# A forgetting-attention kernel with an MLP behind it: the first pair's decay folded into its score product, its f rows repeated by a second queue, batch 1's loads reordered, and slot 4's bank and transposes changed

## The chip, the core and the metric

The kernel runs on one core of a Trainium2 chip. A core has TensorE (PE in the profile: matrix products from SBUF into PSUM), VectorE (DVE), ScalarE (ACT), GpSimd (POOL) and SyncE (SP). Each engine takes its own instructions in order; they wait for one another by semaphores. Loads and stores are DMAs, issued here from GpSimd's queue, from SyncE's and, in the changed kernel, once from ScalarE's; all of them share 16 DMA engines. GpSimd's DMAs convert float32 into float16 on the way. The metric is device time of one execution in microseconds (us), lower is better.

## The reference, cut to what matters

Eight batches of eight heads, 576 positions, 64 numbers per head. Attention with a forget gate f comes first; all heads of a position together are then the 512 inputs of an MLP with a hidden width of 2048, over 8 x 576 = 4608 positions.

```python
scores = scale * np.matmul(q, k.transpose(0, 1, 3, 2))
log_f = np.log(np.clip(f, 0.0001, 1.0))
cum = np.cumsum(log_f, axis=-1)
decay = cum[:, :, :, None] - cum[:, :, None, :]
scores = np.where(causal, -1000000000.0, scores + decay)
...
return np.matmul(attn, v)        # attn: softmax of scores
...
h = x @ w_in
g = h - np.tanh(h)
return g @ w_out
```

The decay of a score depends on its query row by cum of the query's position, and on its key column by minus cum of the key's. So it can be had by a few more rows of the q k product: a row of ones against cum, and so on.

## The kernel before, in words

Work goes by pairs of heads: 8 batches of 4 pairs, 32 pairs in all, and the MLP's products are dealt out between the pairs' own work from pair 4 on. The order on all engines is written out by hand: `start` (L562) for the first pair's opening, `bulk` (L193) for loads, and then, for each slot p (L652), the list that `att_items` (L588) makes. A slot holds the scores of pair p, the values of pair p-1, the transposes of q and k for pair p+1, and the loads that the table LOADS (L208) names by slot and tile. Here slot 4 is the one in which batch 0 ends and batch 1 and the MLP begin.

A pair has seven score tiles (`TILES`, L311): three for its first head, a small one for both heads' last key block (tile 3), three for the second head. `scores` (L328) makes a tile: products of KT (keys) with QT (queries) into a PSUM bank (L348), for batch 0 a product that adds the causal mask (L351), and an exp on ScalarE (L357) from PSUM into SBUF. The tag "sc" has two banks, so a tile waits for the exp of two tiles ago; tile 3 of batch 0 and the dummy products (`unread`, L553) use the bank "tr". `values` (L378) multiplies exps by v (L385), and VectorE divides (L394 to L396). `turn` (L403) transposes the result into XR, for batch 0 by TensorE (L411) and a ScalarE copy (L412). `mlp1` (L432) makes a tile of h (L442), ScalarE its tanh (L447), VectorE the sum gq (L453), which frees h's bank. Banks of the MLP, of the turn and of the early transposes come in turn from three (`m_bank`, L70, with the count M_AT).

For batch 0, q and k come in rows (`load_qk`, L101) and are turned by TensorE (`trans`, L266; products L277, copies out of PSUM by ScalarE L288 or VectorE L290). In the first slots nearly all of VectorE's time is these copies.

KT and QT have 67 rows: 64 of data and three for the decay. The decay starts from f, loaded as 64 rows (L135): clamp (L162), Ln (L169), running sum cum by a scan (L171), its float16 upper part chi (L174), the rest clo (L178) and cq (L565). `load_aug` (L180) puts one row each of chi, clo and cq into rows 64 to 66 by DMA, for batch 0 from GpSimd's queue, and `const_rows` (L187) the constant rows from SyncE's. Pair 0 would be too early for that: its scores use 64 rows of KT and QT, and `decay_part` (L316) adds the decay by two more products for each piece, one with the selector sel over chi and clo (L317), one with a column of the identity over cq (L319). A piece is a block of keys against a run of queries; pair 0 has twelve.

GpSimd's queue holds, in this order: q and k of heads 0 to 3, the identity mask between them (L142), v of heads 0 and 1, q of heads 4 to 7, the three decay rows, k of heads 4 to 7, four blocks of v (`load_v_block`, L130), and then batch 1's q and k, w_in in two halves (`load_win`, L200) and batch 1's v.

The dummy products of L556 read nothing of the problem and nobody reads them; they keep TensorE at work while data is on the way.

Of the kernel before, what the change touches and what calls it, by code (L numbers as in the profile page):

```python
# [21 lines left out]
def kernel(  # L22
# [107 lines left out]
    def load_v_block(b, n, h0, h1):  # L130
# [8 lines left out]
    nc.vector.memset(warm, 1.0)  # L139
    id16 = cst.tile([P, P], FP16)  # L140
# [5 lines left out]
    ones16 = TK[0:NH, 0, :]  # L146
    sel = cst.tile([P, 2], FP16)
    dec = cst.tile([P, PITCH], FP16)
# [5 lines left out]
    nc.vector.memset(dec[:, S:PITCH], 0.0)  # L154
# [6 lines left out]

    nc.vector.tensor_scalar(out=lf, in0=lf, scalar1=0.0001, scalar2=1.0,  # L162
                            op0=ALU.max, op1=ALU.min)

    nc.vector.scalar_tensor_tensor(out=sel, in0=id16[:, 0:2], scalar=-1.0, in1=id16[:, NH:NH + 2],
                                   op0=ALU.mult, op1=ALU.subtract)
    nc.vector.memset(vn[0][D:P, NJ - 1, :, :], 0.0)
    nc.vector.memset(vn[0][:, :, :, D:VW], 1.0)
    nc.scalar.activation(out=lf, in_=lf, func=AF.Ln)  # L169
    cum = TQ[0][0:NH, :, :].rearrange("p c s -> p (c s)").bitcast(FP32)[:, S:2 * S]  # L170
    nc.vector.tensor_tensor_scan(out=cum, data0=ones16, data1=lf, initial=0.0,  # L171
                                 op0=ALU.mult, op1=ALU.add)
    chi = dec[0:NH, 0:S]
    nc.vector.tensor_scalar_mul(out=chi, in0=cum, scalar1=inv_qscale)  # L174
    cq = cst.tile([NH, S], FP16)
    expo = cst.tile([1, 1], FP32)
    clo = dec[NH:2 * NH, 0:S]
    nc.vector.scalar_tensor_tensor(out=clo, in0=cum, scalar=inv_qscale, in1=chi,  # L178
                                   op0=ALU.mult, op1=ALU.subtract)
    def load_aug(b):  # L180
        i, hs = b % 2, slice(b * H, (b + 1) * H)
        eng = nc.gpsimd if b == 0 else nc.sync
        eng.dma_start(out=KT[i][D:D + 1, :, 0:S], in_=chi[hs, :])
        eng.dma_start(out=QT[i][D + 2:D + 3, :, :], in_=cq[hs, :])
        eng.dma_start(out=KT[i][D + 1:D + 2, :, 0:S], in_=clo[hs, :])
# [18 lines left out]
    def load_wout(t0, t1):  # L204
# [111 lines left out]
    def decay_part(ps, a, j, i0, n, col):  # L316
        nc.tensor.matmul(out=ps[:, col:col + n], lhsT=dec[:, j * P:(j + 1) * P],  # L317
                         rhs=sel[:, a:a + 1].to_broadcast([P, n]), start=True, stop=False)
        nc.tensor.matmul(out=ps[:, col:col + n], lhsT=id16[0:NH, a:a + 1].to_broadcast([NH, P]),  # L319
                         rhs=cq[:, i0:i0 + n], start=False, stop=False)  # L320

    FIRST = []

    def decay(ti):
        FIRST.append(ps_sc.tile([P, 512], FP32, tag="sc", name="ps"))
        decay_part(FIRST[0], *TILES[ti][0])

    def scores(b, c, ti):  # L328
        if FIRST:
            ps = FIRST.pop()  # L330
        elif b == 0 and ti == LAST:
# [9 lines left out]
        own = b == 0 and c == 0  # L341
        rows = D if own else D + 3
        for a, j, i0, n, col in TILES[ti]:
            h = 2 * c + a
            if own and ti > 0:
                decay_part(ps, a, j, i0, n, col)
            cut = min(P, n) if b == 0 and i0 == j * P else 0
            nc.tensor.matmul(out=ps[:, col:col + n], lhsT=KT[b % 2][0:rows, h, j * P:(j + 1) * P],  # L348
                             rhs=QT[b % 2][0:rows, h, i0:i0 + n], start=not own, stop=cut == 0)
            if cut:  # L350
                nc.tensor.matmul(out=ps[:, col:col + cut], lhsT=id16, rhs=late[:, 0:cut],  # L351
                                 start=False, stop=True)
# [4 lines left out]
        nc.scalar.activation(out=e[:, lo:hi], in_=ps[:, lo:hi], func=AF.Exp, scale=qscale)  # L357
# [204 lines left out]
    def start():  # L562
        unread(33)
        q_rest = trans(*pairs[0], qn, QT, True, "AAAA", True)
        nc.scalar.activation(out=cq, in_=cum, func=AF.Copy, bias=-SHIFT * inv_qscale, scale=inv_qscale)  # L565
        nc.scalar.activation(out=expo, in_=lf[0:1, 0:1], func=AF.Exp)
        unread(6)
        k_rest = trans(*pairs[0], kn, KT, True, "VVVV", True)
        unread(22)
        decay(0)  # L570
        unread(8)
        scores(*pairs[0], 0)
        for fn in k_rest:
            fn()
        q_rest[0]()
        scores(*pairs[0], 1)
        q_rest[1]()
        for e in EL[0:2]:
            nc.vector.memset(e, 0.0)
        nc.vector.memset(KT[0][:, :, S:PITCH], 0.0)  # L580
# [7 lines left out]
    def att_items(p):  # L588
# [8 lines left out]
        for ti in range(len(TILES)):  # L597
# [5 lines left out]
            if early and p > 0 and ti in (0, 6):  # L603
                put(unread, 2)
# [4 lines left out]
            at_q, at_k = (1, 3) if p == 0 else (0, 1) if early else (0, 2) if p == NPAIR else (0, 3)  # L609
# [37 lines left out]
    FIVE = {PE, mybir.EngineType.Pool, mybir.EngineType.SP, mybir.EngineType.DVE, mybir.EngineType.Activation}  # L647
    with tc.manual_schedule(engines=FIVE):
        start()
    with tc.manual_schedule(engines=FIVE):  # L650
        bulk()
        for p in range(len(pairs) + 1):  # L652
            b, c = divmod(p, NPAIR)
            items = att_items(p)
            take = TAKE[p] if p < len(TAKE) else 8 - (p - len(TAKE)) % 2
            if p == 2 * NPAIR - 1:
                keep()
            if p == 2 * NPAIR + 1:
                KEPT.clear()
                widen(1)  # L660
            mine = mlp[at:at + take]
            at += take
            first = 14 if p == NPAIR else 0
            if p == len(pairs):
                for fn, *args in mine[0:2]:
                    fn(*args)
                mine = mine[2:]
            given, n = 0, 0
            whole = sum(counts for _, counts in items)
            for emit, counts in items:  # L670
                emit()
                n += counts
                while n > first and given < len(mine) and given * (whole - first) < (n - first) * len(mine):
                    fn, *args = mine[given]
                    fn(*args)
                    given += 1
        widen(2)
        for fn, *args in mlp[at:]:
            fn(*args)
# [28 lines left out]
```

## Time and profile before

| what | value |
|---|---|
| median of 3 executions | 344.49 us (344.33 to 344.98) |
| the profiled execution itself | 344.34 us |
| its span in the profile | 342.6 us |
| TensorE busy | 334.8 us, 98% of the span |
| VectorE, ScalarE, GpSimd busy | 261.8, 233.1, 162.3 us |
| first score of pair 0, of pair 1 (chain) | 9.19 us, 16.38 us |
| granted TensorE clock | 0.998 |

Times inside the profile count from the span's start. The chain of waits follows the work that ended last back from the last instruction; a piece "PE ps L348" is a score product, "PE idle L556" a dummy product, "ACT e L357" an exp that TensorE waited for. Busy TensorE need not mean useful TensorE: dummy products count too. The DMA view gives for each issue the time until its last byte has landed.

### The profile page before, as it was taken

What the parts mean: (1) busy time and instruction counts of PE and PEld (TensorE: products, weight loads), DVE (VectorE), ACT (ScalarE), POOL (GpSimd) and SP (SyncE); (2) the same over time, 40 slices, a digit from 0 to 9 for tenths busy, and PEclk for the clock granted to TensorE, in tenths of its full rate; (3) what the DMA queues carried; (4) which work ended last, traced back from release to release, by engine and by line L of the source; (5) the groups of instructions that cost most, each with busy time, mean ns of one, the idle gap of its engine ahead of it and who ended that gap; (6) DMA issues with size and microseconds to landing.
All of it is one profiled execution on the core that took longest, in us unless ns stands there. A gap on an engine that the chain in (4) does not pass through costs nothing.

```text
span 342.6 us, 8607 instructions
## 1 busy us (share of the span) xinstructions
PE 334.8 (98%) x3253; PEld 231.2 (67%) x3253; DVE 261.8 (76%) x504; ACT 233.1 (68%) x437; POOL 162.3 (47%) x319
## 2 busy tenths in 40 slices
PE   8989899999999999999999999999999999999995
PEld 7477455555588557865788888756875586486485
DVE  7599689657898779678867886788667766976874
ACT  5587877898897786778677876787658832732630
POOL 8973665686637763776476557732322220000000
PEclk9999999999999999999999999999999999999999
DMA  9999999999999999999999998990130013002003
GB/s 112 151 170 201 192 203 158 150 137 175 116 124 112 189 128 117 109 178 129 106 112 172 128 124 87 196 127 19 50 110 19 19 49 110 0 29 96 0 15 110
DMA packets 144877, 38.80 MB, mean 113 GB/s; under 512 B 128148, under 2 KB 143236, under 8 KB 144836
## 3 DMA queue, kind: packets, MB, share of 16 engines
q0 software_dynamic: 92480, 18.39, 69.1%
q1 hardware_dynamic: 52356, 19.88, 29.6%
q8 instruction: 25, 0.41, 0.5%
q14 instruction: 16, 0.13, 0.1%
HBM read 36.85 MB, written 9.44 MB: 135 GB/s over the span
## 4 chain that ended last, share of the span: by engine, by line
PE 96%; ACT 2%; DVE 0%; issue 0%; ACTq 0%
PE hps L442 36%; PE ops L507 29%; PE ps L348 13%; PE av L385 8%; PE ops L483 4%; PE idle L556 2%; PE t L277 2%; ACT e L357 1%; PE ps L351 1%; PE ps L319 1%; PE ps L317 0%; PE x L411 0%; ACT th L447 0%; DVE gq L453 0%; ACT XR L412 0%
## 5 line engine op out<-in xcount | busy, mean ns | idle before, releaser
L442 PE MATMUL hps<-XR,win 128*128 128x512 f16 (+1 forms) x640 | 140.9, 357 | 1.5 <-DVE gq L453 0.8
L447 ACT ACTIVATE th<-hps 128x512 f32<-128x512 f32 x144 | 86.7, 602 | 55.7 <-PE hps L442 54.1
L357 ACT ACTIVATE e<-ps 128x512 f16<-128x512 f32 x192 | 110.5, 597 | 13.8 <-PE ps L348 6.1
L453 DVE TENSOR_TENSOR gq<-hps,th 128x512 f16<-128x512 f32 x144 | 98.4, 688 | 26.6 <-ACT th L447 25.1
L367 POOL TENSOR_SCALAR_AFFINE_SELECT e<-e 128x128 f16<-128x128 f16 x168 | 61.3, 366 | 72.3 <-ACT e L357 70.0
L442 PEld LDWEIGHTS <-win 128*128 128x128 f16 x640 | 57.8, 97 | 49.3 <-issue 1.4
L348 PE MATMUL ps<-QT,KT 67*128 67x64 f16 (+5 forms) x384 | 77.9, 276 | 1.7 <-ACT e L357 1.3
L507 PEld LDWEIGHTS <-gq 128*128 128x128 f16 x640 | 60.3, 97 | 11.1
L507 PE MATMUL ops<-wout,gq 128*128 128x256 f16 x512 | 63.2, 272 | 0.0
L348 PEld LDWEIGHTS <-KT 67*128 67x128 f16 (+1 forms) x384 | 36.7, 98 | 24.0 <-issue 1.3
L385 PEld LDWEIGHTS <-e 128*128 128x128 f16 x896 | 32.2, 97 | 3.8
L385 PE MATMUL av<-vn,e 128*128 128x65 f16 x896 | 33.6, 193 | 0.0
L131 POOL DMA_DIRECT2D vn<-in_v_dram x32 | 28.0, 878 | 9.9 <-DMA win<-in_moe_w_in_dram 4.7
L507 PE MATMUL ops<-W,sq 128*128 128x256 f16 x256 | 31.2, 272 | 0.0
L396 DVE TENSOR_TENSOR xn<-av,rs 128x640 f16<-128x640 f32 x32 | 26.4, 825 | 1.1
L507 PEld LDWEIGHTS <-sq 128*128 128x128 f16 x256 | 24.1, 97 | 3.4
L367 POOL TENSOR_SCALAR_AFFINE_SELECT el<-el 128x128 f16<-128x128 f16 x28 | 9.3, 333 | 27.3 <-ACT el L357 26.7
L108 POOL DMA_DIRECT2D kn<-in_k_dram x25 | 21.2, 847 | 1.5 <-issue 1.3
L108 POOL DMA_DIRECT2D qn<-in_q_dram x25 | 21.2, 847 | 1.3 <-issue 0.9
L394 DVE TENSOR_SCALAR rs<-av 128x10 f32<-128x10 f32 x32 | 5.2, 163 | 18.8 <-PE av L385 17.6
L290 DVE COPY QT<-t 64x576 f16<-64x576 f16 x18 | 14.4, 801 | 4.4 <-PE t L277 4.3
L290 DVE COPY KT<-t 64x576 f16<-64x576 f16 (+1 forms) x22 | 16.3, 740 | 1.6 <-PE t L277 1.4
(82 smaller groups left out, 308.7 us busy)
## 6 DMA issues: line engine op xcount, KB each, us to landing
out_dram<-ost SPq DMA_DIRECT2D x34, 256.0 KB
vn<-in_v_dram POOLq DMA_DIRECT2D x24, 128.0 KB, 5.6
qn<-in_q_dram POOLq DMA_DIRECT2D x20, 128.0 KB, 4.4
kn<-in_k_dram POOLq DMA_DIRECT2D x20, 128.0 KB, 4.7
win<-in_moe_w_in_dram POOLq DMA_DIRECT2D x2, 1024.0 KB, 15.0
wout<-in_moe_w_out_dram POOLq DMA_DIRECT2D x2, 1024.0 KB, 14.1
XR<-xn SPq DMA_TRANSPOSE x56
vn<-in_v_dram POOLq DMA_DIRECT2D x12, 64.0 KB, 4.8
```

Of the source, the lines that this page charges most:

```text
L108: nc.gpsimd.dma_start(out=dst[b % 2][0:pn, n, :].rearrange("p (h d) -> p h d", h=H), in_=src[b, :, n * P:n * P + pn, :].rearrange("h p d - ...
L131: nc.gpsimd.dma_start(out=vn[b % 2][:, n, h0:h1, 0:D], in_=v[b, h0:h1, n * P:(n + 1) * P, :].rearrange("h p d -> p h d"))
L290: nc.vector.tensor_copy(out=to, in_=of)
L348: nc.tensor.matmul(out=ps[:, col:col + n], lhsT=KT[b % 2][0:rows, h, j * P:(j + 1) * P], rhs=QT[b % 2][0:rows, h, i0:i0 + n], start=not ow ...
L357: nc.scalar.activation(out=e[:, lo:hi], in_=ps[:, lo:hi], func=AF.Exp, scale=qscale)
L367: nc.gpsimd.affine_select(out=view, in_=view, compare_op=ALU.is_ge, fill=0.0, base=0, pattern=pat, channel_multiplier=-1)
L385: nc.tensor.matmul(out=av[:, a, ib, :], lhsT=E.pop((b, c, a, j, ib)), rhs=vn[b % 2][:, j, 2 * c + a, 0:D + 1], start=(j == 0), stop=(j == ib))
L396: nc.vector.tensor_tensor(out=xn.rearrange("p i (a d) -> p a i d", a=2), in0=av[:, :, :, 0:D], in1=rs.to_broadcast([P, 2, NJ, D]), op=ALU. ...
L442: nc.tensor.matmul(out=hps[:, o:o + n], lhsT=win[:, ci, ft * P:(ft + 1) * P], rhs=XR[:, ci, t:t + n], start=(ci == 0), stop=(ci == NCH - 1))
L447: nc.scalar.activation(out=th, in_=hps, func=AF.Tanh, scale=-1.0)
L453: nc.vector.tensor_tensor(out=GQ[(u, i)][:, half, kt, :], in0=hps, in1=th, op=ALU.add)
L507: nc.tensor.matmul(out=ps[:, m, :], lhsT=LHS[lhs](u, kt // 4)[:, kt % 4, m * P:(m + 1) * P], rhs=rhs[:, kt, :], start=(fresh and (apart or ...
```

## The change

It has four parts.

Pair 0: f is loaded once more, as 24 further rows (each of batch 0's eight heads three times) by ScalarE's queue, so that clamp, Ln, scan and chi run over 88 rows instead of 64. Rows 64 to 87 of two new operands KS and QS (they lie in W1 and W2, which are not used yet) are built in place: on VectorE chi and the rest of it for KS, on ScalarE a scaled and shifted cum for QS (`row_q`), with per-row factors `per` that VectorE makes from columns of the identity. Only the rows of the head in question have factors other than zero in QS. Pair 0's scores then are one product of 88 rows for each piece; `decay_part`, `decay`, `dec` and `sel` are gone. The dummy products are counted anew: 47, 6 and 38 ahead of the first score, 4 behind it, 4 behind the second tile, and 4 each at tiles 5 and 6.

The head of the kernel is also under the hand-written order now; the identity mask stands ahead of the first q and k loads, and several memsets come earlier. The decay rows of batch 0 for the later pairs: chi stays behind q of heads 4 to 7, clo and cq go behind the second of v's four blocks.

Loads of batch 1: q and k of heads 2 and 3 come first, then w_in's first half, then q and k of heads 4 to 7; v and w_in's second half come a few tiles later. In slot 1 the k transposes for pair 2 move from tile 1 to tile 3.

Slot 4: the k transposes move from tile 2's start to behind the turn, the second parts of the first two MLP tiles from tiles 3 and 4 to 4 and 5, and the count of banks goes back by one after the turn of pair 3, so that the next MLP tile takes the turn's bank.

```diff
-    lf = TQ[0][0:NH, :, :].rearrange("p c s -> p (c s)").bitcast(FP32)[:, 0:S]
-    nc.sync.dma_start(out=lf, in_=f.rearrange("b h s -> (b h) s"))
-    load_qk(qn, q, 0, 0, 2)
-    load_qk(kn, k, 0, 0, 2)
+    NX = NH + 3 * H
+    lf = TQ[0][0:NX, :, :].rearrange("p c s -> p (c s)").bitcast(FP32)[:, 0:S]
+    nc.sync.dma_start(out=lf[0:NH, :], in_=f.rearrange("b h s -> (b h) s"))
+    nc.scalar.dma_start(out=lf[NH:NX, :], in_=bass.AP(f.tensor, f.offset, [[S, H], [0, 3], [1, S]]))
...
+    load_qk(qn, q, 0, 0, 2)
+    load_qk(kn, k, 0, 0, 2)
     load_qk(qn, q, 0, 2, 4)
     load_qk(kn, k, 0, 2, 4)
...
+    for to, g in ((isb, 1), (isc, 2)):
+        nc.vector.tensor_reduce(out=to, in_=id16[0:NX, NH + g:NX:3], op=ALU.add, axis=mybir.AxisListType.X)
+    nc.vector.tensor_scalar(out=mul_k, in0=isb, scalar1=-inv_qscale, scalar2=inv_qscale, op0=ALU.mult, op1=ALU.add)
+    nc.vector.tensor_scalar_mul(out=add_k, in0=isb, scalar1=-1.0)
+    nc.vector.tensor_scalar_mul(out=mul_l, in0=isc, scalar1=inv_qscale)
...
+    for h, (mul, add) in enumerate(((mul_0, add_0), (mul_1, add_1))):
+        nc.vector.tensor_scalar_mul(out=mul, in0=column(1, h), scalar1=inv_qscale)
+        nc.vector.scalar_tensor_tensor(out=add, in0=mul, scalar=-SHIFT, in1=column(0, h), op0=ALU.mult, op1=ALU.add)
+        nc.vector.tensor_tensor(out=add, in0=add, in1=column(2, h), op=ALU.subtract)
...
+    nc.vector.tensor_scalar(out=chi, in0=cum, scalar1=mul_k, scalar2=add_k, op0=ALU.mult, op1=ALU.add)
+    nc.vector.scalar_tensor_tensor(out=KS[NH:NX, 0, 0:S], in0=cum[NH:NX, :], scalar=mul_l[NH:NX, :], in1=chi[NH:NX, :],
                                    op0=ALU.mult, op1=ALU.subtract)
...
     def bulk():
+        (k_hi, chi_0), *rest = aug_rows(0)
         load_qk(qn, q, 0, 4, H)
-        load_aug(0)
+        nc.gpsimd.dma_start(out=k_hi, in_=chi_0)
         load_qk(kn, k, 0, 4, H)
         for n in range(NJ - 1):
             load_v_block(0, n, 2, H)
+            if n == 1:
+                for to, of in rest:
+                    nc.gpsimd.dma_start(out=to, in_=of)
...
-             (0, 4): [lambda: load_qk(qn, q, 1, 2, H)],
-             (1, 0): [lambda: load_qk(kn, k, 1, 2, H)],
-             (1, 2): [lambda: load_win(0, DFF // 2)],
-             (1, 5): [lambda: load_v_rest(1), lambda: load_v_head(1, 0)],
-             (2, 1): [lambda: load_v_head(1, 1), lambda: load_win(DFF // 2, DFF)],
+             (0, 4): [lambda: load_qk(qn, q, 1, 2, 4), lambda: load_qk(kn, k, 1, 2, 4)],
+             (1, 0): [lambda: load_win(0, DFF // 2)],
+             (1, 2): [lambda: load_qk(qn, q, 1, 4, H)],
+             (1, 5): [lambda: load_qk(kn, k, 1, 4, H)],
+             (2, 1): [lambda: load_v_rest(1), lambda: load_v_head(1, 0)],
+             (2, 4): [lambda: load_v_head(1, 1), lambda: load_win(DFF // 2, DFF)],
...
-            if own and ti > 0:
-                decay_part(ps, a, j, i0, n, col)
             cut = min(P, n) if b == 0 and i0 == j * P else 0
-            nc.tensor.matmul(out=ps[:, col:col + n], lhsT=KT[b % 2][0:rows, h, j * P:(j + 1) * P],
-                             rhs=QT[b % 2][0:rows, h, i0:i0 + n], start=not own, stop=cut == 0)
+            nc.tensor.matmul(out=ps[:, col:col + n], lhsT=kt[0:rows, h, j * P:(j + 1) * P],
+                             rhs=qt[0:rows, h, i0:i0 + n], start=True, stop=cut == 0)
...
             x32 = m_bank("x32")
+            if c == NPAIR - 1:
+                M_AT[0] -= 1
...
-        unread(33)
-        q_rest = trans(*pairs[0], qn, QT, True, "AAAA", True)
-        nc.scalar.activation(out=cq, in_=cum, func=AF.Copy, bias=-SHIFT * inv_qscale, scale=inv_qscale)
-        nc.scalar.activation(out=expo, in_=lf[0:1, 0:1], func=AF.Exp)
+        unread(47)
+        row_q(0, mul_0, add_0)
+        q_rest = trans(*pairs[0], qn, (QS,), True, "AAAA", True)
+        nc.scalar.activation(out=cq, in_=cum[0:NH, :], func=AF.Copy, bias=-SHIFT * inv_qscale, scale=inv_qscale)
         unread(6)
-        k_rest = trans(*pairs[0], kn, KT, True, "VVVV", True)
-        unread(22)
-        decay(0)
-        unread(8)
+        k_rest = trans(*pairs[0], kn, (KS,), True, "VVVV", True)
+        unread(38)
         scores(*pairs[0], 0)
+        row_q(1, mul_1, add_1)
+        unread(4)
+        nc.vector.scalar_tensor_tensor(out=clo, in0=cum[0:NH, :], scalar=inv_qscale, in1=chi[0:NH, :], op0=ALU.mult, op1=ALU.subtract)
+        nc.vector.tensor_copy(out=KS[NH:NX, 1, 0:S], in_=KS[NH:NX, 0, 0:S])
...
-            if early and p > 0 and ti in (0, 6):
-                put(unread, 2)
+            if early and ti in (0, 6) or p == 0 and ti == 5:
+                put(unread, 2 if p else 4)
...
-            at_q, at_k = (1, 3) if p == 0 else (0, 1) if early else (0, 2) if p == NPAIR else (0, 3)
+            at_q, at_k = (1, 3) if p == 0 else (0, 3) if p == 1 else (0, 1) if early else (0, 2) if p == NPAIR else (0, 3)
...
-                if ti in (3, 4):
-                    put(mlp1, 0, ti - 3, 1)
-            if ti == at_k and p < 2 * NPAIR - 1:
+                if ti in (4, 5):
+                    put(mlp1, 0, ti - 4, 1)
+            if ti == at_k and p < 2 * NPAIR - 1 and p != NPAIR:
                 put(trans, *after, kn, KT, early, "VV")
...
                     put(mlp1, 0, 1, 0)
                     put(turn, *before)
+                    put(trans, *after, kn, KT, early, "VV")
```

More of the change, by code (lines that the diff above doesn't have):

```diff
@@ L143 @@
                             fill=1.0, base=0, pattern=[[-1, P]], channel_multiplier=1)
+    load_qk(qn, q, 0, 0, 2)
+    load_qk(kn, k, 0, 0, 2)
     load_qk(qn, q, 0, 2, 4)
     load_qk(kn, k, 0, 2, 4)
-    ones16 = TK[0:NH, 0, :]
-    sel = cst.tile([P, 2], FP16)
-    dec = cst.tile([P, PITCH], FP16)
+    ones16 = TK[0:NX, 0, :]
     nc.vector.memset(ones16, 1.0)
@@ L153 @@
     nc.vector.memset(late, 0.0)
-    nc.vector.memset(dec[:, S:PITCH], 0.0)
+    nc.vector.memset(KT[0][:, :, S:PITCH], 0.0)
+    chi = cst.tile([NX, S], FP16)
+    clo = cst.tile([NH, S], FP16)
+    cq = cst.tile([NH, S], FP16)
+    KS = W1.rearrange("p k e -> p (k e)")[:, 0:2 * PITCH].rearrange("p (a n) -> p a n", a=2)
+    QS = W2.rearrange("p k e -> p (k e)")[:, 0:2 * S].rearrange("p (a n) -> p a n", a=2)
+    nc.vector.memset(KS[0:NX, :, S:PITCH], 0.0)
+    per = cst.tile([NX, 9], FP32)
+    nc.vector.memset(vn[0][D:P, NJ - 1, :, :], 0.0)
+    isb, isc, mul_k, add_k, mul_l, mul_0, add_0, mul_1, add_1 = (per[:, i:i + 1] for i in range(9))
     EL = [cst.tile([P, 192], FP16, tag=f"el{i}", name=f"el{i}") for i in range(3)]
@@ L162 @@
+    for e in EL[0:2]:
+        nc.vector.memset(e, 0.0)
     nc.vector.tensor_scalar(out=lf, in0=lf, scalar1=0.0001, scalar2=1.0,
                             op0=ALU.max, op1=ALU.min)
-    nc.vector.scalar_tensor_tensor(out=sel, in0=id16[:, 0:2], scalar=-1.0, in1=id16[:, NH:NH + 2],
-                                   op0=ALU.mult, op1=ALU.subtract)
-    nc.vector.memset(vn[0][D:P, NJ - 1, :, :], 0.0)
     nc.vector.memset(vn[0][:, :, :, D:VW], 1.0)
+    for h, (mul, add) in enumerate(((mul_0, add_0), (mul_1, add_1))):
+        nc.vector.tensor_scalar_mul(out=mul, in0=column(1, h), scalar1=inv_qscale)
+        nc.vector.scalar_tensor_tensor(out=add, in0=mul, scalar=-SHIFT, in1=column(0, h), op0=ALU.mult, op1=ALU.add)
+        nc.vector.tensor_tensor(out=add, in0=add, in1=column(2, h), op=ALU.subtract)
@@ L169 @@
     nc.scalar.activation(out=lf, in_=lf, func=AF.Ln)
-    cum = TQ[0][0:NH, :, :].rearrange("p c s -> p (c s)").bitcast(FP32)[:, S:2 * S]
+    nc.scalar.activation(out=expo, in_=lf[0:1, 0:1], func=AF.Exp)
+    cum = TQ[0][0:NX, :, :].rearrange("p c s -> p (c s)").bitcast(FP32)[:, S:2 * S]
     nc.vector.tensor_tensor_scan(out=cum, data0=ones16, data1=lf, initial=0.0,
                                  op0=ALU.mult, op1=ALU.add)
-    chi = dec[0:NH, 0:S]
-    nc.vector.tensor_scalar_mul(out=chi, in0=cum, scalar1=inv_qscale)
@@ L175, with aug_rows @@
[L175 to L178, printed above, removed]
+    nc.vector.tensor_scalar(out=chi, in0=cum, scalar1=mul_k, scalar2=add_k, op0=ALU.mult, op1=ALU.add)
+    nc.vector.scalar_tensor_tensor(out=KS[NH:NX, 0, 0:S], in0=cum[NH:NX, :], scalar=mul_l[NH:NX, :], in1=chi[NH:NX, :],
                                    op0=ALU.mult, op1=ALU.subtract)
+    def aug_rows(b):
+        i, hs = b % 2, slice(b * H, (b + 1) * H)
+        return [(KT[i][D:D + 1, :, 0:S], chi[hs, :]), (KT[i][D + 1:D + 2, :, 0:S], clo[hs, :]), (QT[i][D + 2:D + 3, :, :], cq[hs, :])]
@@ L180, in load_aug @@
     def load_aug(b):
[L181 to L185, printed above, removed]
+        for to, of in aug_rows(b):
+            nc.sync.dma_start(out=to, in_=of)
     def const_rows(i):
@@ L314 @@
              4: (0, 1, 1, P), 5: (0, 1, 1, P), 6: (0, 2, 320, P)}
[L316 to L326, printed above, removed]
     def scores(b, c, ti):
-        if FIRST:
-            ps = FIRST.pop()
-        elif b == 0 and ti == LAST:
+        if b == 0 and ti == LAST:
             ps = ps_tr.tile([P, UW], FP32, tag="tr", name="ps")
@@ L576, in start @@
         scores(*pairs[0], 1)
+        unread(4)
         q_rest[1]()
-        for e in EL[0:2]:
-            nc.vector.memset(e, 0.0)
-        nc.vector.memset(KT[0][:, :, S:PITCH], 0.0)
     def last():
@@ L646 @@
     at = 0
[L647 to L679, printed above, removed]
+    start()
+    bulk()
+    for p in range(len(pairs) + 1):
+        b, c = divmod(p, NPAIR)
+        items = att_items(p)
+        take = TAKE[p] if p < len(TAKE) else 8 - (p - len(TAKE)) % 2
+        if p == 2 * NPAIR - 1:
+            keep()
+        if p == 2 * NPAIR + 1:
+            KEPT.clear()
+            widen(1)
+        mine = mlp[at:at + take]
+        at += take
+        first = 14 if p == NPAIR else 0
+        if p == len(pairs):
+            for fn, *args in mine[0:2]:
+                fn(*args)
+            mine = mine[2:]
+        given, n = 0, 0
+        whole = sum(counts for _, counts in items)
+        for emit, counts in items:
+            emit()
+            n += counts
+            while n > first and given < len(mine) and given * (whole - first) < (n - first) * len(mine):
+                fn, *args = mine[given]
+                fn(*args)
+                given += 1
+    widen(2)
+    for fn, *args in mlp[at:]:
+        fn(*args)
 _INS = ['q', 'k', 'v', 'f', 'moe_w_in', 'moe_w_out']
```

11 lines of the change are left out of this document (9 added, 2 removed).

## The prediction

> **What bounds the kernel now.** I read the page's engine line and its chain first, then the chain of the first 45 us in order of time, then the waits of that stretch, then timelines engine by engine, and last the DMA issues with their times to landing.
>
> ```profile
> PE 334.8 (98%) x3253; PEld 231.2 (67%) x3253; DVE 261.8 (76%) x504; ACT 233.1 (68%) x437; POOL 162.3 (47%) x319
> ...
> PE 96%; ACT 2%; DVE 0%; issue 0%; ACTq 0%
> ```
>
> TensorE is the bound, and from 36.7 us to the end it hardly pauses, so whatever the first 37 us gain or lose goes to the end nearly whole. There the waits are these (waiter, what it waited for, total, times, longest):
>
> ```profile
> DVE QT L290 <- PE t L277: 3.1, 2, 2.3
> ...
> PE ps L348 <- ACT e L357: 1.3, 3, 0.5
> ...
> PE hps L442 <- DVE gq L453: 0.8, 1, 0.8
> ...
> PE hps L442 <- ACT XR L412: 0.7, 1, 0.7
> ```
>
> Two of them lie in slot 4 (the passage from batch 0 to batch 1). The chain there in order of time (start, length, what):
>
> ```profile
> 33.90 0.29 PE x L411 x5
> ...
> 34.21 0.66 ACT XR L412
> ...
> 34.91 0.39 PE hps L442
> ...
> 35.33 0.61 ACT th L447
> ...
> 35.95 0.70 DVE gq L453
> ...
> 36.70 1.02 PE hps L442 x4
> ```
>
> The reader sees TensorE twice with nothing to do: until the copy XR ends (0.68 idle before 34.91), and until gq of the first MLP tile frees its bank (0.75 before 36.70).
>
> In the first pair, of which the chain shows, among others,
>
> ```profile
> 9.19 0.32 PE ps L348
> ...
> 13.15 0.22 PE ps L317
> 13.37 0.32 PE ps L319
> 13.69 0.21 PE ps L348
> 13.90 0.16 PE ps L351
> ...
> 16.38 0.22 PE ps L348
> ```
>
> TensorE itself is the limit: each score piece costs three products (L317, L319, L348), 7.19 us from the first score at 9.19 to the second pair's first at 16.38. Behind it VectorE stands idle 2.27 us, and then runs almost without a gap to 33.45:
>
> ```profile
> 17.06 1.63 DVE L290 COPY QT<-t 64x576 f16<-64x576 f16 x2 [2.27 <-PE t L277]
> ```
>
> So what the front is worth is read at one point: when pair 1's first score starts (16.38), since the q transposes of pair 2 and that copy follow it at once.
>
> **Part by part: pair 0 itself.** Removed are 24 decay products. In the chain L317 adds up to 1.54 us and L319 to 2.58; two of the 24 (0.28 and 0.32) lie ahead of 9.19, so 3.5 us leave the stretch. L351 took 0.16 beside the short weights and 0.06 in pair 1, where all weights have 67 rows; ten of them save 1.0. Twenty new dummy products (2 took 0.11) add 1.1. TensorE's work falls from 7.19 to about 3.8 us, and other engines set the pace.
>
> First score: VectorE gets 13 more small operations ahead of the scan. Ahead of the clamp stand the KT memset (0.27, now early), two el memsets (0.24 together) and five one-column operations (no such row; from 0.07, the pitch of sel, to 0.25, a dependent rs; I take 0.14): 1.2 us, of which the 0.66 that VectorE waited for f covers half. Six more stand between clamp and scan, 0.9 to 1.5, under a cover of about 0.5 (Ln 0.68 less hand-overs). I put the scan 0.9 late; sel (0.16) is gone behind it. The first copies of k end near 9.6 instead of 8.8. TensorE's dummies agree: 47 at 112 ns (33 took 3.70) end at 6.4, and with 6, two sets of transposes and 38 at 55 to 70 ns the first score comes at 9.8, 0.6 later. The f rows by ScalarE's queue (one issue, about 0.6 like SyncE's) come under the table load and the clamp's new delay: nothing. Exp's table load (1.28) now lies between Ln and the scan's end: hidden; without that cover it would cost itself.
>
> ScalarE from there: first exp at 10.3 (0.52 behind the score as before), then exp at 0.55, one added row build (24x576; cq, 64x576, took 0.66), two q copies (0.47), el 0.28: the last exp starts near 14.8, where it was 16.41. VectorE: clo 0.75, a row copy (0.2 to 0.75; I take 0.3, nearest to a small f16 operation), k copies 0.97, then QT 1.61 and KT 1.60 of pair 1: 14.8. By these, pair 1 could score at 14.9, 1.5 earlier.
>
> **The rows by DMA.** Pair 1 needs its three decay rows in KT and QT by DMA from GpSimd's queue. Before, the three were issued at 7.70, 8.22 and 8.74 and landed by 13.5, far ahead of 16.38. Now chi stays where it was, but clo and cq go behind the rest of k and two blocks of v.
>
> ```profile
> KT<-dec POOLq DMA_DIRECT2D x1, 9.0 KB, 4.8
> ...
> kn<-in_k_dram POOLq DMA_DIRECT2D x1, 288.0 KB, 6.5
> ...
> vn<-in_v_dram POOLq DMA_DIRECT2D x1, 96.0 KB, 6.4
> ...
> vn<-in_v_dram POOLq DMA_DIRECT2D x3, 96.0 KB, 6.2
> ```
>
> (last figure: us from issue to landing; the rows are clo at 8.74, the rest of k at 9.24, v's first block at 9.92, and the group of the second at 10.76.) On GpSimd the identity mask (0.32) now comes ahead of the first loads, which start 0.25 late; with chi ready near 7.6, k goes out at 8.3, the v blocks at 9.0 and 9.9, clo at 10.7 (clo itself ready near 10.4), cq at 11.2. At the 4.8 us of the small row cq lands at 16.0; behind the second v block, which landed at 16.96, it lands near 17.0. A GpSimd wait on a landing took some 0.2 to 0.3 us more, so pair 1 starts between 16.2 and 17.2. The small row is nearest in kind, the block in place: I take 16.6. Against 16.38 the front then loses 0.2; its ends are a gain of 1.5 (rows no limit, 14.9) and a loss of 0.8.
>
> [...]
>
> **What moves with it.** Pair 2's k transposes (0.26) go behind the fourth tile of pair 1. TensorE had them in the time that it now waits for an exp, so score 4 of pair 1 comes 2.7 us behind its first either way; VectorE is busy with QT (1.63) until then: 0 to 0.3 loss, taken as 0. The half of win now passes q and k of heads 4 to 7 of batch 1 (576 KB, some 3.5 us by the 2.7 us between the landings of two 432 KB loads), so it lands near 28, and was needed at 32.1. What it passed is needed in slot 5, past 42. The v loads and win's second half, also moved a few tiles, keep their place in the byte order. GpSimd holds an issue until the eighth DMA before it lands (the fourth block of v goes out at 12.94, behind q at 12.6); pair 4's first k load then goes out near 15.3 instead of 14.4 and lands near 20, needed at 26. SyncE's constant rows and batch 1's rows change order only; nobody waits for them before 29. Had win landed with the rest as before (30.8), a front 1.5 us earlier would still just have met it.
>
> **Slot 4.** The k transposes move behind the turn, so the turn starts at 33.64 (divide ends at 33.45), XR ends near 34.6, and transposes (0.26) and tiles 3 and 4 (0.28) fill most of the wait. With the count stepped back, the third MLP tile takes the turn's bank, free at 34.6, in place of that which waits for gq: it starts at 35.3 instead of 36.70. Its successor now waits for gq, and VectorE has the moved KT copies (1.6) ahead of it: gq ends at 36.5, the fourth tile starts at 36.6 instead of 37.94. Gain 1.3; ends 0.7 (gq's wait only) and 1.43 (both holes).
>
> **Sum.** The profiled execution took 344.34 (span 342.6, 1.7 around it), 0.15 under the median of 344.49. 344.34 + 0.2 - 1.3 = 343.2.
>
> **Rivals.** A measurement here tells 0.2% (0.7 us) from nothing.
> First, the rows are no limit (for: they are 9 KB; against: they were behind the big block before): pair 1 at 14.9, 344.34 - 1.5 - 1.3 = 341.5.
> Second, they land strictly behind the second v block: pair 1 at 17.2, 344.34 + 0.8 - 1.3 = 343.8.
> Third, on the other side: they land with the last v block, which landed at 18.24 (issued at 12.94), because the queue is already late by the first loads and the f rows. Pair 1 at 18.5 costs 2.1: 345.1. From 17.9 on it eats slot 4's gain.
> Fourth, the clock: TensorE has work for only 3.8 of the 6 to 7 us ahead of pair 1, and then waits. In the first 5 us dummies took 112 ns, later 70 and less; at the slow rate pair 1's 2.7 us would double: 343.2 + 2.7 = 345.9. Against it: holes of 0.7 us left no slow products behind them. [...]
>
> **The numbers.** My forecast (pair 1 between 15.6 and 16.9, 342.2 to 343.6) 0.38; first rival 0.25; second 0.18; third 0.10; fourth 0.09. Faster: the forecast, the first, and 0.05 of the second, 0.68; same: 0.13 of the second and 0.02 of the third, 0.15; slower 0.17. The range, 341.3 to 344.7, leaves out part of the first and most of the last two.
>
> **What would show it.** Right: no L317 or L319; the first score near 9.8; VectorE's copy of pair 2 within 0.5 us of 17.06, with TensorE idle before it until clo and cq land at 16 to 17; in slot 4 the third tile's products 1.3 us nearer to the turn, and the wait for XR under 0.3. Wrong: pair 1 scoring near 15 (then 341.5), slow products in pair 1, TensorE waiting for win or for v, or a wait for gq as long as before.

## The result, and the profile after

The changed kernel takes 345.61 us (median of 22 runs, 344.13 to 348.46), the kernel before 344.49 (22 runs, 344.33 to 345.94). The ratio is 1.0044, 95% interval 1.0028 to 1.0059: slower by 0.44%, where 343.2 us and a gain were forecast, and 0.9 us above the upper end of the range. The times of the changed kernel fall into steps that go with the mean clock granted to TensorE in each run: 344.13 at 1.000 (one run), 344.8 to 345.8 at 0.993 to 0.995 (12), 346.3 to 346.6 at 0.990 (5), 347.7 to 348.5 at 0.985 (4). A step of 0.005 of the clock is 1.7 us of the 344 lost, so 3.4 us at half rate. By that working the nine runs at 0.990 and 0.985 had two or three such stretches; none of them was profiled, so where the further ones lie stays open. Further down, one run of `rows_sp` (349.50 us) counts as slow, being over 1.5% above that kernel's fastest, and is left out of its ratio.

The profiled run took 345.54 us (span 343.8), 1.20 over that of before. Of its page, the row of TensorE and the row of the granted clock in 40 slices of 8.6 us, and the chain by engine:

```profile
PE   8598999999999999999999999999999999999996
...
PEclk9989999999999999999999999999999999999999
...
PE 92%; DMA 3%; POOL 2%; ACT 2%; issue 0%; DVE 0%; ACTq 0%
```

The chain was 96% TensorE before; now the DMA and GpSimd's issues ahead of it hold 5%. TensorE's second slice (8.6 to 17.2 us) is half empty, and in the third the clock is not full. A stretch in which TensorE has nothing to do is called a hole here. The waits of the first 45 us (waiter, what it waited for, total, times, longest):

```profile
PE ps L358 <- DMA qn<-in_q_dram: 2.3, 1, 2.3
...
DVE QT L317 <- PE t L304: 3.3, 2, 3.1
...
PE ps L358 <- ACT W L315: 1.2, 1, 1.2
...
PE hps L454 <- ACT XR L424: 0.2, 1, 0.2
```

Slot 4's two holes have gone, all but 0.2 of the wait for XR, as the change meant. In their place TensorE waits 2.25 us for a transfer ahead of pair 1 (L358 is now the score product). The profile names q, but the first score of pair 1 reads KT and QT with their decay rows, and it starts just after those have landed. VectorE's longest wait for its copy QT grows from 2.3 to 3.1. Inside pair 0, ahead of 12.51, TensorE has another hole of 1.19 us, until ScalarE's copy W is done; it comes up again below. The transfers of the rows (queue, KB, us from issue to landing; clo issued at 10.29, cq at 10.81):

```profile
KT<-clo POOLq DMA_DIRECT2D x1, 9.0 KB, 6.0
...
QT<-cq POOLq DMA_DIRECT2D x1, 9.0 KB, 5.9
```

cq lands at 16.7. What follows is in the chain in order of time (start, length, what):

```profile
16.92 0.38 PE ps L358
...
18.84 0.83 PE av L395 x15
...
20.36 0.83 PE av L395 x15
...
22.88 0.26 PE ps L358
...
24.83 0.45 PE av L395 x15
...
35.97 0.29 PE x L423 x5
...
36.28 0.66 ACT XR L424
...
36.98 0.38 PE hps L454
...
37.58 1.08 PE hps L454 x5
...
41.29 0.86 PE hps L454 x4
```

and in the kernel before, for comparison:

```profile
20.70 0.25 PE ps L348
...
40.15 0.86 PE hps L442 x4
```

Pair 1 starts at 16.92, 0.54 later than the 16.38 of before. Its values part (L395, 15 products) takes 0.83 us where pair 2's takes 0.45: the same products at about half rate. Pair 2 starts at 22.88, 2.18 later than the 20.70 of before, so 1.64 more was lost inside pair 1. From the MLP products that were at 40.15 and are now at 41.29 the order is the same again in both kernels. They are 1.14 late, so between pair 2 and there 1.04 of the 2.18 has come back. 0.54 + 1.64 - 1.04 is 1.14, of the 1.20. The clock, by stretches of 3.4 us laid so that one begins where the clock falls (busy us and products of PE, then PEld, DVE, ACT, POOL, and then PEclk, DMA share, GB/s):

```profile
14.55:17.95 3.40, 1.15 (x16) 0.81 (x14) 0.34 (x2) 1.09 (x2) 2.69 (x5) 0.99 1.70 130
17.95:21.35 3.40, 3.37 (x47) 2.96 (x45) 2.35 (x4) 1.51 (x4) 3.29 (x8) 0.51 0.89 132
21.35:24.75 3.40, 3.00 (x42) 2.44 (x41) 3.00 (x6) 2.87 (x6) 3.08 (x5) 1.00 1.11 194
```

One stretch of 3.4 us at half rate stands between two at full rate. It begins 1.0 us after TensorE has work again, not in the hole itself.

### The profile page after: what moved, and what is told of

It reads as the page before. It is cut to its first block, busy times and chain, and to the rows that moved or that the text cites. A ratio compares the mean times of both kernels' runs of the same rounds, so it can differ in the third digit from the quotient of the medians.

```text
span 343.8 us, 8658 instructions
## 1 busy us (share of the span) xinstructions
PE 333.1 (97%) x3271; PEld 232.6 (68%) x3271; DVE 263.9 (77%) x516; ACT 234.9 (68%) x440; POOL 161.5 (47%) x321
## 4 chain that ended last, share of the span: by engine, by line
PE 92%; DMA 3%; POOL 2%; ACT 2%; issue 0%; DVE 0%; ACTq 0%
PE hps L454 36%; PE ops L519 28%; PE ps L358 13%; PE av L395 9%; PE ops L495 4%; DMA qn<-in_q_dram 3%; PE t L304 1%; ACT e L367 1%; PE ps L361 0%; POOL vn L127 0%; POOL qn L102 0%; POOL kn L102 0%; PE x L423 0%; POOL vn L131 0%; ACT XR L424 0%
## 5 line engine op out<-in xcount | busy, mean ns | idle before, releaser
L377 POOL TENSOR_SCALAR_AFFINE_SELECT e<-e 128x128 f16<-128x128 f16 x168 | 59.6, 356 | 74.8 <-ACT e L367 72.3
L358 PE MATMUL ps<-QT,KT 67*128 67x512 f16 (+1 forms) x372 | 74.9, 278 | 4.0 <-DMA qn<-in_q_dram 2.3
L358 PEld LDWEIGHTS <-KT 67*128 67x128 f16 x372 | 35.6, 98 | 26.2 <-issue 3.9
L395 PEld LDWEIGHTS <-e 128*128 128x128 f16 x896 | 33.1, 98 | 3.9
L395 PE MATMUL av<-vn,e 128*128 128x65 f16 x896 | 34.4, 194 | 0.0
L534 ACT ACTIVATE m<-ops 128x512 f32<-128x512 f32 x16 | 9.5, 596 | 10.9 <-PE ops L519 10.9
```

What stands on the lines that cost most here:

```text
L358: nc.tensor.matmul(out=ps[:, col:col + n], lhsT=kt[0:rows, h, j * P:(j + 1) * P], rhs=qt[0:rows, h, i0:i0 + n], start=True, stop=cut == 0)
L395: nc.tensor.matmul(out=av[:, a, ib, :], lhsT=E.pop((b, c, a, j, ib)), rhs=vn[b % 2][:, j, 2 * c + a, 0:D + 1], start=(j == 0), stop=(j == ib))
```

## The experiments

Two questions were put. Is the loss the clock, and does the clock fall for the hole (theory), or for the thinner work of pair 0 (rival)? And why do the rows land so late: because of the v blocks ahead of them (theory A), or because they are built later (theory B)?

**Filling the hole with dummy products.** Run `warm`:

```diff
-put(unread, 2 if p else 4)
+put(unread, 2 if p else 4 if ti < 6 else 38)
```

> The changed kernel with 38 dummy products instead of 4 behind pair 0's last tile, so that TensorE works through most of the wait for the rows; the rows stay late. Theory: pair 1 still starts near 17.0, but the clock stays up, values of pair 0 take 0.45 us a part instead of 0.83, and slot 4's gain is seen in full: 345.5 - 1.6 = 343.9, between 343.6 and 344.4, with little spread from run to run. Rival 1 (the thin stretch from 10 to 14 us is what lowers the clock): the slow rate stays, about 345.5. Rival 2 (the loss has nothing to do with the clock): 345.5, or later by what the dummies overrun.

Measured: 344.01 us (11 runs, 343.64 to 344.74; ratio to before 0.9989, 0.9980 to 0.9997). TensorE's timeline around pair 1's first score (start, us, line, form, count):

```profile
14.29 2.28 PE L568 MATMUL idle<-warm 128*128 128x128 f16 x38
16.51 0.38 PE L358 MATMUL ps<-QT,KT 67*128 67x512 f16 x1
```

Its chain has pair 0's values at full rate again:

```profile
18.12 0.46 PE av L395 x15
...
18.96 0.45 PE av L395 x15
```

34 useless products more, with the rows issued where they were, take 1.6 us off the median and most of the spread, and every run was granted 0.998 or more. The thin stretch of pair 0 was left as it was, so the rival falls: it is the hole. In this profiled run pair 1 also started at 16.51 for 16.92, so the rows had landed by then, ahead of the 16.7 in the changed kernel's, and not all of the 1.90 between these two profiled runs is the clock.

**A hole alone, in the kernel before.** Run `before_late3` puts two of the three row transfers behind the v blocks while pair 0 keeps all its products:

```diff
-load_aug(0)
+i, hs = 0, slice(0, H)
+nc.gpsimd.dma_start(out=KT[i][D:D + 1, :, 0:S], in_=chi[hs, :])
 load_qk(kn, k, 0, 4, H)
 for n in range(NJ - 1):
     load_v_block(0, n, 2, H)
+    if n == 3:
+        nc.gpsimd.dma_start(out=KT[i][D + 1:D + 2, :, 0:S], in_=clo[hs, :])
+        nc.gpsimd.dma_start(out=QT[i][D + 2:D + 3, :, :], in_=cq[hs, :])
```

> The kernel before, with the rows of clo and cq issued behind all four blocks of v of batch 0, while pair 0 keeps its decay products, so TensorE is busy without a gap until 16.4 and then waits for rows that land near 18.5: a hole of about 2.1 us, as long as that of the changed kernel, behind a full stretch of work. If a hole of that length is enough, the clock falls behind it: 344.4 + 2.1 + 1.2 to 1.6 = 347.7 to 348.1, with spread. If the thin work of the 4 us ahead of the hole is needed too, products behind it stay fast: 346.5, little spread. If the rows land by 17.2 all the same, under 345.5 and nothing is told.

Measured: 347.41 us (6 runs, 345.48 to 349.69; ratio 1.0082, 1.0052 to 1.0112). TensorE's wait, and its clock by stretches in that kernel's profile:

```profile
17.76 0.38 PE L352 MATMUL ps<-QT,KT 67*128 67x512 f16 x1 [1.36 <-DMA qn<-in_q_dram]
```

```profile
15.85:19.25 3.40, 2.04 (x28) 1.47 (x27) 0.65 (x1) 1.57 (x3) 3.28 (x6) 1.00 1.16 148
19.25:22.65 3.40, 3.25 (x43) 2.64 (x41) 3.26 (x7) 1.83 (x5) 3.40 (x7) 0.50 1.27 191
22.65:26.00 3.35, 3.35 (x68) 2.96 (x68) 2.49 (x4) 3.18 (x7) 2.25 (x3) 1.00 1.14 211
```

The rows landed earlier than expected (by 17.76 and not 18.5), and yet a hole of 1.36 us behind full work brought 3.4 us at exactly half rate, 1.5 us after its end. Two of the six runs were granted 1.000, and these took 345.5 and 345.7, which fits the wait alone.

**That hole filled.** Run `late3_warm` adds 22 dummy products there.

> The kernel before with the rows of clo and cq behind all four blocks of v, and 22 dummy products (1.2 us) behind pair 0's last tile, where TensorE waited 1.36 us for the rows. If a single hole of 1.36 us in full work lowers the clock, filling it gives back 1.2 to 1.7 us and leaves the wait alone: 344.4 + 1.4 = 345.8, with little spread. If the half rate there had another cause: about 347.4 as without the dummies.

Measured: 345.60 us (6 runs, 345.43 to 346.79; ratio 1.0033, 1.0021 to 1.0046), with a clock of 0.999 or 1.000 in all six. As expected, the late start remains (pair 1 at 17.46 in the profiled run, 1.08 later than in the kernel before), and there is no half rate.

**A smaller hole.** Run `before_late2` has the rows behind three blocks.

> The kernel before with the rows of clo and cq behind three blocks of v instead of four: they land near 17, and TensorE waits 0.4 to 0.8 us for them behind full work. If the half rate needs a hole longer than about 1 us (holes of 0.7 left none in the kernel before, one of 1.36 did), the time is the wait alone: 344.8 to 345.2, with little spread. If any hole at this place brings it: 346 to 346.6.

Measured: 345.27 us (10 runs, 344.62 to 349.28; ratio 1.0032, 1.0002 to 1.0062). In the profiled run the hole was larger than meant, and left the clock at 1.000:

```profile
17.32 0.38 PE L352 MATMUL ps<-QT,KT 67*128 67x512 f16 x1 [0.93 <-DMA qn<-in_q_dram]
```

Two of its ten runs, 347.12 and 349.28, were granted 0.995 and 0.985. Together, by the granted clock: the kernel before has no hole over 0.75 us from its first dummy product on in its profile, and none of its 66 runs taken beside these was granted less than 0.998. With about 1.4 us four of six fell, with 2.25 us 21 of 22. In between, length alone does not order the runs. `warm`, and below `rows_early` (twice), `old_loads` and `early_el` all hold the hole of 1.18 or 1.19 us inside pair 0 in their profiles, and none of their 33 runs was granted less than 0.998; here two of ten fell, with holes that no trace shows and that may have been longer than 0.93. No sharp length was found.

**Slot 4 by itself.** Run `slot4_only` is the kernel before with the three edits of slot 4:

```diff
 x32 = m_bank("x32")
+if c == NPAIR - 1:
+    M_AT[0] -= 1
...
-if ti in (3, 4):
-    put(mlp1, 0, ti - 3, 1)
+if ti in (4, 5):
+    put(mlp1, 0, ti - 4, 1)
...
 put(turn, *before)
+put(trans, *after, kn, KT, early, "VV")
```

> The kernel before with the edits of slot 4 alone: the bank counter stepped back at the turn, pair 5's k transposes behind the turn, the second parts of the first MLP tiles one tile later. Theory: the gain that the changed kernel shows there, 1.0 to 1.1, comes whole: 344.4 - 1.05 = 343.4, between 343.1 and 343.7. Rival (the gain in the changed kernel is an effect of the earlier landing of win and of its late front, not of these edits): 344.0 to 344.5.

Measured: 343.25 us (8 runs, 343.21 to 343.84; ratio 0.9973, 0.9962 to 0.9983), 1.13 under the 344.38 of before beside it. In its chain:

```profile
33.64 0.33 PE x L413 x5
33.97 0.27 PE t L277 x6
...
35.91 0.70 DVE gq L455
...
36.66 1.02 PE hps L444 x4
```

The turn at 33.64 and the products behind gq at 36.66 are where the prediction had them (33.64 and 36.6); the rival falls. This part is a gain by itself, and the rest of the change loses more than it.

**The rows from SyncE's queue.** Run `rows_sp` issues clo's and cq's rows of batch 0 there:

```diff
-nc.gpsimd.dma_start(out=to, in_=of)
+nc.sync.dma_start(out=to, in_=of)
```

> The changed kernel with clo's and cq's rows of batch 0 issued from SyncE's queue instead of GpSimd's, so that they stand behind no block of v. Theory (the late rows leave TensorE a hole of 2.25 us ahead of pair 1, and for that hole the clock falls to half): the rows land by 14.5, pair 1 scores when KT's copies end, 14.8 instead of 16.92; no product behind it at the slow rate; 345.5 - 2.1 - 1.6 = 341.8, between 341.4 and 342.4, and little spread. Rival 1 (the thin work of pair 0 brings the clock down whatever the rows do): pair 1 at 14.8 but its products slow, about 343.4, with spread. Rival 2 (rows from SyncE queue behind the same bulk in the DMA engines): they land at 16 or later, 344 to 345.5 as now.

Measured: 343.55 us (12 runs, 342.43 to 349.50; ratio 0.9975, 0.9958 to 0.9992). The profiled run is one of the late ones (345.0):

```profile
9.82 0.62 SPq L224 DMA_DIRECT2D KT<-clo  x1
10.49 0.63 SPq L224 DMA_DIRECT2D QT<-cq  x1
```

```profile
16.63 0.44 PE L358 MATMUL ps<-QT,KT 67*128 67x512 f16 x1 [1.71 <-DMA QT<-cq]
```

The rows stand behind nothing large on SyncE's queue, and still TensorE's wait for cq ended only at 16.63 here, as rival 2 had it, and the clock was 0.53 from 17.0 to 20.4. Other runs took 342.4 to 342.8 (5 of 12); none of these was profiled. Passing to another queue gives the rows a chance, not a place.

**Dummies on top of that.** Run `sp_warm`: 24 dummy products instead of 4 with the rows on SyncE's queue.

> The changed kernel with the rows from SyncE's queue and 24 dummy products instead of 4 behind pair 0's last tile (1.1 us more of work in TensorE's wait). If the spread of the run with SyncE's queue alone (342.4 to 345.0) was the clock, it goes and the time is that run's lowest or a little over it: 342.4 to 342.9. If the spread came from the rows' landing, it stays: median 343.5.

Measured: 344.12 us (10 runs, 343.21 to 347.35; ratio 0.9994, 0.9972 to 1.0016). A miss, between the two theories' times. In the profiled run the dummies end near 16.3 and pair 1 starts behind them at 16.29. By this they would also hold pair 1 back in runs whose rows come early, which made the 342.4; no such run was profiled. Nine of the ten runs were granted 0.997 or more and still spread from 343.2 to 344.5; the tenth (0.995) took 347.35. So both the landing and the clock seem to be in the spread of `rows_sp`.

**clo built earlier.** Run `clo_first`, rows on SyncE's queue, clo ahead of the copies of k on VectorE.

> The changed kernel with clo built on VectorE ahead of the first copies of k instead of behind them, and both rows issued from SyncE's queue, at about 8.8 and 9.4. The first score comes 0.75 us later, near 9.8. Theory B (time from issue decides): the rows land 1.0 us earlier than the 16.6 of the run with SyncE's queue alone, near 15.5; pair 1 at 15.6, TensorE's hole about 0.8 us, and the clock mostly stays: 342.5 to 343.3. Theory A (what stands ahead of them): blocks of v are ahead of them in no queue in either run, so they land as late as there, 16 to 16.6: 343.5 or more.

Measured: 342.60 us (10 runs, 342.37 to 346.44; ratio 0.9967, 0.9940 to 0.9994). Six runs took 342.4 to 342.7, so the median lies in the range of theory B and below that of theory A. The profiled run took 345.68, and shows the other kind:

```profile
8.80 0.62 SPq L224 DMA_DIRECT2D KT<-clo  x1
9.47 1.75 SPq L224 DMA_DIRECT2D QT<-cq  x1
```

```profile
17.12 0.38 PE L358 MATMUL ps<-QT,KT 67*128 67x512 f16 x1 [1.78 <-DMA QT<-cq]
```

cq's issue, which takes 0.63 elsewhere, took 1.75, and the wait for cq ended at 17.12, later than the 16.63 of `rows_sp`, where it was issued 1.0 later. So a fixed time from issue (theory B) doesn't hold in this run, although the median alone would speak for it. The v blocks were issued from 8.65 to 12.04 in that run, beside the rows.

**The rows ahead of the v blocks.** Run `rows_early` keeps GpSimd's queue and has it wait for clo:

```diff
 load_qk(kn, k, 0, 4, H)
+for to, of in rest:
+    nc.gpsimd.dma_start(out=to, in_=of)
 for n in range(NJ - 1):
     load_v_block(0, n, 2, H)
-    if n == 1:
-        for to, of in rest:
-            nc.gpsimd.dma_start(out=to, in_=of)
```

> The changed kernel with clo's and cq's rows of batch 0 ahead of all four blocks of v on GpSimd's queue (it now waits for clo, built at 9.8, before it issues the blocks). Theory A (blocks of v ahead of the rows make them late): with only q and k of heads 4 to 7 ahead, which landed by 14.2, they land near 14.5, pair 1 scores near 14.9, and the time is 342.0 to 342.8. Theory B (rows take some 6 us from issue to landing on any queue while the DMA engines work off the bulk, and are late because clo and cq are built 1 to 2 us later than in the kernel before): clo issued at 9.8 and cq at 10.3 land at 16.0 to 16.3, pair 1 near 16.3, a hole of 1.5 us or more and the slow clock stay, 344 to 345.5.

Measured: 342.74 us (4 runs, 342.38 to 343.00; ratio 0.9943, 0.9928 to 0.9958). GpSimd's issues, and then the chain:

```profile
10.24 0.52 POOL L221 DMA_DIRECT2D KT<-clo  x1 [1.40 <-DVE clo L587]
10.80 0.52 POOL L221 DMA_DIRECT2D QT<-cq  x1
11.31 3.34 POOL L131 DMA_DIRECT2D vn<-in_v_dram  x4
```

```profile
14.63 0.22 PE idle L567 x4
14.88 0.39 PE ps L357
```

cq was issued at 10.80, as in the changed kernel (10.81), and pair 1 scored at 14.88 without a wait: cq had landed 4.1 us after its issue or sooner, instead of 5.9. Of the bulk ahead of it only the v blocks are different: theory A, and theory B's 16.0 or later falls. The runs on SyncE's queue suggest, without proof, that v blocks issued beside the rows on another queue can do the same. The same kernel once more, beside the next two:

> The kernel with the rows ahead of the blocks of v once more, to stand beside the next two on the same chip: 342.4 to 343.0, with pair 1's first score near 14.85 and no half rate.

Measured: 342.29 us (4 runs, 342.14 to 343.08; ratio 0.9937, 0.9920 to 0.9955). The profiled run, at 343.08, started pair 1 at 15.36, 0.5 later than expected, behind a wait of 0.49. The profile names an exp; pair 1's copies of k on VectorE had ended at 14.83. A later landing of cq would explain the wait, but was not shown. Over the eight runs of this version the median is 342.5: 1.9 us under the kernel before and 3.1 under the changed one, with nothing added, so it beats both, and `slot4_only` too.

**The loads of batch 1.** Run `old_loads` is `rows_early` with these loads in the order of before.

> The kernel with the rows ahead of the blocks of v, with the loads of batch 1 in the order of the kernel before: q and k of heads 2 to 7 ahead of the first half of win. Theory (win was moved forward so that an earlier front meets it): win lands some 3 to 3.5 us later than the 28 of the run with the new order, near 31.3, where the first MLP product now wants it near 30.8; TensorE waits 0 to 1 us: 342.7 to 343.8, and a wait for win shows. Rival (the order of these loads never matters): 342.7, the same within 0.2.

Measured: 343.55 us (10 runs, 342.47 to 344.43; ratio 0.9963, 0.9947 to 0.9979), 1.0 over the eight runs with the new order. TensorE's timeline in the profiled run (343.05) and the transfer (issued at 17.26):

```profile
31.27 0.82 PE L452 MATMUL hps<-XR,win 128*128 128x512 f16 x3 [0.56 <-DMA win<-in_moe_w_in_dram]
```

```profile
win<-in_moe_w_in_dram POOLq DMA_DIRECT2D x1, 1024.0 KB, 14.0
```

The new order is worth something only once the front is early; in the changed kernel win landed at 27.95 and was wanted after 34. The wait of 0.56 accounts for the profiled run; the rest of the 1.0 was not located.

**VectorE's chain.** Run `early_el` moves the two memsets of el from VectorE to GpSimd.

> The kernel with the rows ahead of the blocks of v, with the two memsets of el (0.25 us together) taken from VectorE ahead of the clamp to GpSimd, where it waits for clo. If VectorE's unbroken chain from 0.9 to pair 1's copies of k, which end at 14.7, sets pair 1's start, that start comes 0.25 earlier, near 14.6: 342.3 to 342.6. If the rows of f on ScalarE's queue (1.38 us of issue from 0.81) land only near 3.7, the clamp waits for them instead and nothing is gained: 342.7.

Measured: 342.55 us (4 runs, 342.23 to 343.44; ratio 0.9944, 0.9925 to 0.9964), no different from the 342.29 beside it. VectorE now waits for what it had been late for:

```profile
3.90 0.61 DVE L183 TENSOR_SCALAR TQ<-TQ 88x576 f32<-88x576 f32 x1 [0.27 <-DMA TQ<-in_f_dram]
```

So the last rows of f land near 3.9 in that run: the second theory of that expectation. Which of f's two transfers is the last, this line does not tell.

## Why the prediction was wrong

The step that failed is the clock. It counts for nothing in the forecast's sum and stands as the fourth rival, at a chance of 0.09; against it stood only that holes of 0.7 us had left no slow products behind them. The runs showed a fall behind the hole of 2.25 us in 21 of 22 runs, 1.64 us lost by it in the profiled one, and no fall once the hole was filled (`warm`) or taken away (`rows_early`): every run of these two was granted 0.998 or more.

- **The hole was in the forecast's own numbers.** It had TensorE's work down to 3.8 us and pair 1 starting at 16.6; the second and third rivals had it later still. With its last exp starting near 14.8, when TensorE's products of pair 0 are done, all three contain a hole of 1.8 us or more behind pair 0. The clock was set beside these cases as a case of its own, when it should have been laid on each of them. A fall within it would have put the forecast at 343.2 + 1.6 = 344.8.
- **Why 0.7 us was the wrong measure.** Holes of 0.7 that left no slow products say nothing of 2 us. In the runs 1.19 us inside pair 0 brought no fall in 33, and 1.36 us behind full work brought one in four of six: about twice the 0.7 was enough there. The length of the half rate did not follow that of the hole: it was 3.4 us behind 2.25 us (17.95 to 21.35 in the changed kernel) and behind 1.36 us (19.25 to 22.65 in `before_late3`).
- **Its price**, "2.7 us would double", was too high: 1.64. The fall came 1.0 us after pair 1's first score and lasted 3.4 us; 3.4 us at half rate lose 1.7.
- **The rows** were the limit, as predicted, and pair 1 was 0.3 later: 16.92 for 16.6. That it was so near is in part luck: cq took 5.9 us to land and not 4.8, but was issued at 10.81 and not 11.2. It landed at 16.7. This is some 0.8 behind the second v block (issued near 9.5, landed near 15.9): the order of the second rival, at a time between it and the forecast.
- **The first rival** (341.5, rows no limit) is what `rows_early` makes true: pair 1 at 14.88 for 14.9. Its time is 342.3 to 342.7, some 1 us more than worked out. Its front is 1.23 ahead of that of `slot4_only` at a score product in slot 4, behind the turn (34.99 for 36.22), and the profiled runs differ by 0.85; 0.17 of the rest is a wait of the k transposes at 56.86, and what remains was not located.
- **The first score** was to be 0.6 late (9.8) and came at 9.05, 0.1 early. The dummies that were to agree with 9.8 were no support: 47 of them took 4.27 us (91 ns each, 112 assumed) and were done by 5.4, not 6.4. The scan started at 5.01, 0.2 later than before and not 0.9: VectorE's wait for f in the kernel before, 0.7, and Ln covered nearly all of the 13 small operations, of which the one-column ones took 0.09 to 0.16.
- **f's issue from ScalarE's queue** took 1.38 us and not 0.6. "Nothing" held all the same, with no cover left: `early_el` shows VectorE waiting for f as soon as its clamp could start 0.25 earlier.
- **VectorE's path to pair 1** ended at 14.71 for 14.8, though its row copy took 0.65 for 0.3 (in `rows_early2` it took 0.30); ScalarE's last exp of pair 0 started at 14.48 for 14.8.
- **Slot 4** was right in its places, and mis-sized by 0.2: 1.13 by itself, 1.04 in the changed kernel, for 1.3.
- **win** landed at 27.95 (28 predicted). "A front 1.5 us earlier would still just have met it" in the old order failed by 0.56 us of wait: win landed at 31.27 there, not 30.8.
- That moving pair 2's k transposes costs nothing was not tried by itself.

By these sizes the sum with full clock is 344.34 + 0.54 - 1.1 = 343.8. The changed kernel's one run at 1.000 took 344.13, and `warm` 344.01. With 1.64 for one stretch at half rate it is 345.4, the middle of the largest group.

## What to carry to other kernels

When a change takes work from TensorE, work out the length of the hole that is left behind it, and lay the price of a falling clock on every case that has such a hole: here a 2.25 us wait cost 1.6 us more than itself. A small transfer that the next stage waits for belongs ahead of the bulk in time: moved behind bulk loads, and in some runs beside them on another queue, 9 KB came about 2 us later (by 14.88 in `rows_early`; at 16.7 in the changed kernel, and with waits until 16.63 and 17.12 in the profiles of `rows_sp` and `clo_first`). Where a hole can't be avoided, dummy products that end when the data arrive can pay (1.6 us here); on top of rows that came early in some runs, they gave nothing (`sp_warm`).

## What the runs showed that was not expected

- Half rate begins 0.2 to 1.5 us after the hole's end (16.8 behind 16.63 in `rows_sp`, 19.25 behind 17.76 in `before_late3`) and lasts 3.4 us in each of the four profiles that show it (the changed kernel, `rows_sp`, `before_late3`, `clo_first`), so the slow products stand away from their cause; a reader who looks only at the hole sees 0.54 of the 2.18.
- Busy time doesn't settle it: the 3.4 us before the fall held 2.04 us of TensorE work in `before_late3`; in the changed kernel the stretch one further back (11.15 to 14.55) held 2.06 and the clock stayed at 1.00 after it. There the longest hole was 1.19, and 1.36 in the other. What decides the fall stays open.
- The same two 9 KB transfers on SyncE's queue beside GpSimd's bulk came, from run to run, early enough for 342.4 us or held pair 1 until 17.12, and once the issue of one took 1.75 us instead of 0.63.
